# Retention attention feeding a top-2 mixture of experts: planner lanes, later expert weights, payloads stored by their own transfer, one-hots by token column

## The chip, the cores and the metric

The kernel runs on one core of a Trainium2 chip. The metric is the device time of one execution in microseconds (us). The core has five instruction queues that run in order, each for itself, and meet through semaphores: PE (matrix products), DVE (VectorE), ACT (ScalarE), POOL (GpSimd) and SP (SyncE, which here only issues transfers). ACT and POOL issue transfers as well. SP and ACT share eight completion semaphores for their transfers, used in turn: each transfer waits for the one eight places before it to land.

## The reference

Eight batches, eight heads, 576 positions, 64 numbers a head. The first part is attention without a softmax: scores fade with the distance by a fixed factor per head, and later positions are cut off. Its result, with the heads laid side by side, is the input `x` (4608 tokens of 512 numbers) of a mixture of eight experts, of which each token uses two.

```python
# attention
scores = scale * np.matmul(q, k.transpose(0, 1, 3, 2))
gamma = 1.0 - 2.0 ** (-5.0 - np.arange(H, dtype=np.float32))
Dmat = np.where(rel >= 0, gamma[:, None, None] ** rel[None, :, :], 0.0)
x = np.matmul(scores * Dmat, v)          # then (batch, position) x (head, d)
# experts
noisy_logits = x @ w_gate + np.log1p(np.exp(x @ w_noise)) * noise
top2 = np.argpartition(-noisy_logits, 2, axis=1)[:, :2]
top2_w = softmax over the two logits
for e in range(E):
    for k in range(2):
        mask = top2[:, k] == e
        h = np.maximum(x[mask] @ w1[e], 0.0)
        out[mask] += top2_w[mask, k, None] * (h @ w2[e])
```

Each expert has 512 x 1024 and 1024 x 512 weights (4 MB in f32, 33.5 MB for the eight).

## The kernel before

**The planner.** Nothing is issued as the code is read. `Plan.op` (L54-216) records each operation with the engines that may run it, an assumed cost, what it reads and writes, and a priority. `Plan.run` (L110) then plays the program through with these costs, picks for each operation the engine that would end it first, gives out buffers, and emits the operations in the order of the planned start times. That order is all that reaches the chip: each engine's queue runs in it, and semaphores keep the data right. `after=` makes the planner hold an operation back until another has ended by the plan; it adds no semaphore. So a change of an assumed cost or of `after` changes the order of instructions in the queues, and nothing else.

**The attention part** runs over 16 units; a unit is one batch and four heads, and four units make a batch pair. `load` (L377) issues five transfers of a unit on SP, 1.5 MB: k in two halves, q, v in two halves. `load_tail` (L395) fetches the last 64 positions of a batch pair in six transfers of 128 KB. `cast` (L406) turns them to bf16 on ACT, DVE and POOL (L420-L435), `tr` (L440) transposes on PE (L453), `scores` (L459, matmuls L478, mask on DVE L486), `states` (L493, L509) and `out_` (L521, L541 and L551) give x, transposed in `xT`. `tail` (L564) does the last 64 positions of a pair: casts on POOL (L578), transposes (L587), scores (L600), mask (L605).

**The routing** (`route`, L632) runs once for a batch pair, that is for 1152 tokens laid out as 128 partitions x 9 token columns, after the pair's last unit. Its steps in order: logits on PE (L652); exponential and logarithm on ACT (L658, L659); a chain of small DVE and POOL operations that picks the two best experts, ending in the one-hot of experts `MM` (L688); the payload `pay` of eight f32 a token (weights and indices, L695-L750); ranks within each expert by prefix-sum matmuls on PE (L716, L718); another chain on DVE (L725-L745) that turns a rank into a slot of the expert's list, split in a low part `lof` (0 to 127) and a high part `hif` (0 to 79). Then the list of tokens of each expert is built by matrix products. For each of the two choices j there is a one-hot `olo` of the low part (nine columns x 128, L757), a one-hot `oh` of the high part (nine columns x 80, L760), both on DVE in one instruction for all nine columns, and `oh` is multiplied by the token numbers `vals` (L763, on POOL or DVE). Nine matmuls per j sum olo^T oh (L769), and L776-L782 turn the sum into the int32 list `xi`.

The rows of x are stored to a table `xd` in device memory for later gathers. For each of five groups of token columns PE transposes them back (L793), ACT or DVE copies them to a buffer `xr` (L798), POOL or DVE copies the payload beside them (L799), and a transfer on ACT's queue stores both (L802): 264 numbers of f32 a row, 256 for x in bf16 pairs and 8 of payload.

**The experts.** `weights` (L851) brings experts 0 to 2 by casting transfers on POOL (L859, L863; four of 1 MB f32 each), held back in the plan until the loads of the units in `WAIT` have landed (L1122-L1124), and experts 3 to 7 on SP (L873, L876) with casts on ACT or DVE. Tokens of an expert are taken in tiles of up to two times 128. Nine tiles of experts 0 to 2 whose tokens are known early (`CLOSE`, `tiles` L882) run within the attention part, for pairs 0 to 2; the rest follows after pair 3's list. For each tile `fetch` (L903) gathers rows of `xd` on POOL (L913) and transposes them (L922); a gather waits for all row stores of the pairs that it may read (`xd_done`, in `record`, L1085). `up` (L961, matmuls L979), `down` (L999, L1014) follow; `finish` (L1047) scales the result by the token's weight on ACT (L1061) or DVE (L1063) and stores it to a table `yd` by SP (L1067), or, where it is a token's second expert, adds the first one's row (L1042 gathers it on POOL, L1071 adds on DVE) and scatters to the output on POOL (L1075).

Of the kernel before, what the change touches and what calls it, by code (L numbers as in the profile page):

```python
# [8 lines left out]
F32 = mybir.dt.float32  # L9
F16 = mybir.dt.float16  # L10
BF16 = mybir.dt.bfloat16
# [18 lines left out]
YOFF = [sum(min(-(-x // P) * P, CAP) for x in FIRST[:e]) for e in range(E + 1)]  # L30
WAIT = (8, 11, 14)
CLOSE = ((256, 0, 0, 0, 0, 0, 0, 0), (512, 384, 384, 0, 0, 0, 0, 0), (768, 640, 512, 0, 0, 0, 0, 0))
# [21 lines left out]
class Plan:  # L54
# [55 lines left out]
    def run(self):  # L110
        free, dma_free = {}, {}
        head = {k: 0 for k in self.fifo}
        used = {}
        ready = [o for o in self.ops if not o.need]
        order = []
# [24 lines left out]
        while ready:  # L140
            pick = None
            for o in ready:
# [76 lines left out]
class Kernel:  # L219
    def __init__(self, tc, ctx, src, gates, noise, w1, w2, out, xd, yd):  # L220
# [40 lines left out]
    def setup(self):  # L261
# [62 lines left out]
        for b in range(2):  # L324
# [49 lines left out]
    def unit(u):  # L374
        return u // 4, u // 2 % 2, u % 2

    def load(self, u):  # L377
        pl, nc = self.pl, self.nc
        bp, hq, b = self.unit(u)
        d = self.u[u] = {}  # L380
        for n in "kqv":
            t = d["raw" + n] = pl.buf("big", "att")
            s = self.src[n][2 * bp + b, 4 * hq:4 * hq + 4]
            if n == "q":
                pl.op("SP", 0.07, lambda e, s=s, t=t: nc.sync.dma_start(
                    out=t.t.rearrange("p (h x) -> p h x", h=4), in_=s[:, :512].rearrange("h (p r) d -> p h (r d)", r=4)),
                    w=[t], prio=u, dma=1.6)
            else:
                for c in range(2):
                    pl.op("SP", 0.07, lambda e, s=s, t=t, c=c: nc.sync.dma_start(  # L390
                        out=t.t.rearrange("p (c h x) -> p c h x", c=2, h=4)[:, c],
                        in_=s[:, 256 * c:256 * c + 256].rearrange("h (p r) d -> p h (r d)", r=2)),
                        w=[(t, c)], prio=u, dma=0.96)

    def load_tail(self, bp, prio):  # L395
        pl, nc = self.pl, self.nc
        d = self.tails[bp] = {}
        for n in "kqv":
            t = d["raw" + n] = pl.buf("half", "tl")
            for b in range(2):  # L400
                pl.op("SP", 0.07, lambda e, n=n, t=t, b=b: nc.sync.dma_start(
                    out=t.t[b * HD:(b + 1) * HD].rearrange("p (h d) -> p h d", h=E),
                    in_=self.src[n][2 * bp + b, :, 512:, :].rearrange("h s d -> s h d")),
                    w=[(t, b)], prio=prio, dma=0.8)

# [226 lines left out]
    def route(self, bp, prio):  # L632
# [104 lines left out]
        for j, op in ((0, Alu.add), (1, Alu.subtract)):  # L737
            o("DVE", DV, lambda e, j=j, op=op: V.tensor_tensor(gli.t[:, j], bt.t[:, j], t()[:, j], op), [bt, kt], [(gli, j)])
        lo, hi, lof, hif = f("lo", [P, 2, C], I32), f("hi", [P, 2, C], I32), f("lof", [P, 2, C], F16), f("hif", [P, 2, C], F16)
        ov = f("ov", [P, 2, C])  # L740
# [15 lines left out]
        for j in range(2):  # L756
            o("DVE", 1.3, lambda e, j=j: V.tensor_tensor(  # L757
                olo.t[:, j], iota.t.unsqueeze(1).to_broadcast([P, C, P]), lof.t[:, j].unsqueeze(2).to_broadcast([P, C, P]),
                Alu.is_equal), [iota, lof], [(olo, j)])
            o("DVE", 0.9, lambda e, j=j: V.tensor_tensor(  # L760
                oh.t[:, j], iota.t[:, :NH].unsqueeze(1).to_broadcast([P, C, NH]),
                hif.t[:, j].unsqueeze(2).to_broadcast([P, C, NH]), Alu.is_equal), [iota, hif], [(oh, j)])
            o({"DVE": 0.9, "POOL": 1.4}, 0, lambda e, j=j: self.eng(e).tensor_tensor(  # L763
                oh.t[:, j], oh.t[:, j], vals.t.unsqueeze(2).to_broadcast([P, C, NH]), Alu.mult), [vals, (oh, j)], [(oh, j)])
        pT = self.psum("rt")
# [19 lines left out]
        for g in ((0, 2), (2, 2), (4, 2), (6, 2), (8, 1)):  # L785
# [3 lines left out]
            def rows(e, c=c, n=n, p=p):  # L789
# [7 lines left out]
            o({"ACT": 0.17 + 0.43 * n, "DVE": 0.15 + 0.28 * n}, 0, lambda e, n=n, p=p, xr=xr: self.copy(  # L797
                e, xr.t.bitcast(BF16)[:, :n, :DM], p.t.bitcast(BF16).rearrange("p (c d) -> p c d", c=2)[:, :n]), [p], [(xr, 0)])  # L798
            o({"POOL": 0.3, "DVE": 0.2}, 0, lambda e, c=c, n=n, xr=xr: self.eng(e).tensor_copy(  # L799
                xr.t[:, :n, DM // 2:], pay.t[:, c:c + n, :]), [pay], [(xr, 1)])  # L800
# [284 lines left out]
    def record(self):  # L1085
        pl = self.pl
        self.u, self.tails, self.T, self.xT, self.W, self.t, self.keep, self.scats, self.wdma = {}, {}, {}, {}, {}, {}, {}, {}, []
        self.setup()
# [237 lines left out]
```

## Time and profile before

| | us |
|---|---|
| three runs | 522.32, 524.5, 525.01 |
| median | 524.5 |
| profiled execution | 519.78 |
| its span (first to last instruction) | 518.2 |
| mean granted PE clock in it | 0.927 |
| PE busy | 435.5 (84%) |
| POOL busy | 298.2 (58%) |
| DVE busy | 222.4 (43%) |
| ACT busy | 209.7 (40%) |

The span falls in two. From 0 to about 205 us run the 16 units, the four routings and the nine early tiles; pair 3's list is ready at 202 us. From there on PE has only the experts. In a timeline row the columns are the start, the duration of the group, the engine, the line, the operation, output<-input, shape and count, and in brackets the idle time of the engine before it and what ended it. In a waits row stand the waiting engine and line, what it waited for, and the total, the number of times and the longest, in us. A suffix q (SPq) means the engine's instruction queue: the time it was held at an instruction that only issues a transfer. "issue" is time for which the trace shows no cause.

### The profile page before, as it was taken

The numbers are of one execution on the slowest core, as the hardware profiler recorded it, in microseconds if no ns is written. First come the engines' busy times: TensorE is split into PE (matmuls) and PEld (weight loads), VectorE is DVE, ScalarE is ACT, GpSimd is POOL, SyncE is SP. The second block draws the span as 40 slices with busy tenths as digits, with TensorE's granted clock in tenths as the row PEclk, the third lists the DMA queues.
The fourth block names the chain that finished last, engine by engine and source line by source line (L and its number), as shares of the span: only waits on it lengthen the run. The fifth ranks groups of instructions, "written<-read, shape, count | busy, mean of one in ns | idle before, by whom it ended". The sixth has DMA issues, their size and how long they took to land.

```text
span 518.2 us, 12025 instructions
## 1 busy us (share of the span) xinstructions
PE 435.5 (84%) x4784; PEld 296.4 (57%) x4784; DVE 222.4 (43%) x535; ACT 209.7 (40%) x345; POOL 298.2 (58%) x355
## 2 busy tenths in 40 slices
PE   1887639876798899899999889989997799988993
PEld 1665527664576666567565546645645465654661
DVE  2465597793649359411515152341251121312132
ACT  3465425753565454345435334342441222322311
POOL 8846794795677527513253555546447366666453
PEclk9999757987969579999999999999999799999998
DMA  8999999999765314427679864885865333444333
GB/s 242 226 273 231 310 277 267 295 274 294 162 138 99 109 60 143 146 76 246 250 247 372 280 199 134 297 281 162 281 256 175 104 127 120 146 162 132 124 123 104
DMA packets 92125, 102.91 MB, mean 199 GB/s; under 512 B 21502, under 2 KB 70143, under 8 KB 92066
## 3 DMA queue, kind: packets, MB, share of 16 engines
q1 hardware_dynamic: 71874, 60.36, 38.7%
q0 software_dynamic: 15264, 36.89, 26.8%
q10 hardware_dynamic: 4928, 4.87, 2.8%
q8 instruction: 38, 0.62, 0.5%
q14 instruction: 21, 0.17, 0.1%
HBM read 83.20 MB, written 26.63 MB: 212 GB/s over the span
## 4 chain that ended last, share of the span: by engine, by line
PE 46%; issue 15%; POOL 11%; DMA 11%; DVE 7%; SPq 4%; ACT 3%; another core or an unknown queue 1%; POOLq 0%; ACTq 0%; DVEq 0%
PE ps L1014 15%; PE ps L979 14%; DMA xg<-xd,xi 4%; PE ps L509 4%; POOL xg L913 3%; DMA out_dram<-half,xg 3%; POOL half L1042 2%; DMA half<-in_q_dram 2%; PE ps L922 2%; PE ps L453 2%; PE ps L541 2%; PE ps L478 2%; POOL out_dram L1075 2%; SPq L390 2%; DMA big<-in_k_dram 1%
## 5 line engine op out<-in xcount | busy, mean ns | idle before, releaser
L979 PE MATMUL ps<-half,W 128*128 128x256 bf16 (+2 forms) x1344 | 221.2, 264 | 10.2 <-issue 6.1
L1014 PE MATMUL ps<-W,half 128*128 128x512 bf16 x624 | 222.7, 387 | 3.3 <-issue 1.8
L979 PEld LDWEIGHTS <-W 128*128 128x128 bf16 x1344 | 122.4, 98 | 79.9 <-issue 24.1
L993 ACT ACTIVATE half<-ps 128x512 bf16<-128x512 f32 (+2 forms) x160 | 87.1, 558 | 174.2 <-PE ps L979 108.8
L913 POOL DMA_INDIRECT xg<-xd,xi x80 | 83.2, 1040 | 104.9 <-DMA out_dram<-half,xg 24.9
L1014 PEld LDWEIGHTS <-half 128*128 128x128 bf16 x624 | 61.6, 100 | 34.0 <-issue 17.5
L1075 POOL DMA_INDIRECT out_dram<-half,xg x39 | 39.2, 1006 | 33.2 <-DVE half L1071 16.9
L1071 DVE SCALAR_TENSOR_TENSOR half<-ps,xg,half 128x512 f32<-128x512 f32 (+1 forms) x39 | 27.7, 745 | 68.0 <-issue 24.2
L1042 POOL DMA_INDIRECT half<-yd,xg x39 | 39.1, 1002 | 11.9 <-issue 11.6
L486 DVE TENSOR_TENSOR half<-ps,mask 128x512 bf16<-128x512 f32 x64 | 40.2, 708 | 6.5 <-ACT half L1061 3.2
L254 DVE COPY half<-ps 128x1024 bf16<-128x1024 bf16 (+2 forms) x47 | 30.9, 661 | 22.1 <-PE ps L922 8.7
L252 ACT ACTIVATE half<-ps 128x1024 bf16<-128x1024 bf16 (+2 forms) x31 | 29.4, 969 | 24.6 <-POOL oh L763 7.2
L428 POOL TENSOR_TENSOR half<-big,tab 128x1024 bf16<-128x1024 f32 x15 | 29.5, 1964 | 14.8 <-PE ps L551 5.9
L922 PE MATMUL ps<-ident__69,xg 128*128 128x128 bf16 (+1 forms) x320 | 28.7, 225 | 8.7 <-DMA xg<-xd,xi 7.4
L509 PE MATMUL ps<-half,half 64*64 64x64 bf16 (+2 forms) x512 | 32.4, 239 | 2.5 <-issue 1.9
L453 PE MATMUL ps<-ident__69,half 128*128 128x128 bf16 x256 | 24.9, 271 | 9.0 <-ACT half L420 6.0
L922 PEld LDWEIGHTS <-xg 128*128 128x128 bf16 (+1 forms) x320 | 21.4, 102 | 18.2 <-DMA xg<-xd,xi 10.0
L435 POOL TENSOR_TENSOR half<-big,tab 128x512 bf16<-128x512 f32 x26 | 28.4, 1106 | 0.5 <-issue 0.5
L509 PEld LDWEIGHTS <-half 128*64 128x64 bf16 (+1 forms) x512 | 20.1, 117 | 15.0 <-issue 7.2
L252 ACT ACTIVATE tb<-ps 64x512 bf16<-64x512 f32 x30 | 17.7, 591 | 26.4 <-PE ps L509 12.6
L1063 DVE TENSOR_SCALAR half<-ps,xg 128x512 f32<-128x512 f32 x9 | 6.8, 750 | 49.6 <-issue 32.7
L453 PEld LDWEIGHTS <-half 128*128 128x128 bf16 x256 | 21.3, 126 | 10.0 <-ACT half L420 6.0
(173 smaller groups left out, 436.9 us busy)
## 6 DMA issues: line engine op xcount, KB each, us to landing
big<-in_moe_w_dram SPq DMA_DIRECT2D x40, 512.0 KB
yd<-half SPq DMA_DIRECT2D x40, 256.0 KB
big<-in_k_dram SPq DMA_DIRECT2D x32, 256.0 KB
big<-in_q_dram SPq DMA_DIRECT2D x16, 512.0 KB
big<-in_v_dram SPq DMA_DIRECT2D x32, 256.0 KB
W<-in_moe_w_dram POOLq DMA_DIRECT2D x12, 512.0 KB
xd<-xr ACTq DMA_DIRECT2D x16, 264.0 KB
xg<-xd,xi POOLq DMA_INDIRECT x80
```

What stands on the lines that cost most here:

```text
L252: self.nc.scalar.activation(out, in_, Act.Copy)
L254: self.eng(e).tensor_copy(out, in_)
L453: nc.tensor.transpose(v[:, hp, x, :], i[:, y, hp * P:(hp + 1) * P], ident.t)
L486: nc.vector.tensor_tensor(S.t.bitcast(BF16).rearrange("p (h c x) -> p h c x", h=2, c=2)[:, h], p[h].t.rearrange("p (c x) -> p c x", c=2), ...
L509: nc.tensor.matmul(o[h * HD:(h + 1) * HD, hp, n, :], lhsT=kv[0][:k, r, c, 2 * hp + h, :], rhs=m, start=(hp == 0 and c == 0 and k == P and ...
L913: pl.op("POOL", 1.3, lambda _, x=x, h=h, n=n: nc.gpsimd.indirect_dma_start(out=x.t[:n, :], out_offset=None, in_=self.xd[:rows, :], in_offs ...
L922: nc.tensor.transpose(pv()[:, di, s * P:s * P + n], xb[:, di * P:(di + 1) * P], ident.t[:n, :n])
L979: nc.tensor.matmul(pv()[:, f2, :], lhsT=w.t[:, o:o + P], rhs=xv()[:, di, :n], start=(di == 0), stop=(di == KD - 1))
L993: nc.scalar.activation(hv(), pv(), Act.Relu)
L1014: nc.tensor.matmul(po[s].t[:n], lhsT=hv[:, s * P:s * P + n], rhs=w.t[:, o:o + DM], start=(f == 0), stop=(f == KF - 1))
L1042: pl.op("POOL", 1.3, lambda _, b=b, iy=iy, n=self.size(j): nc.gpsimd.indirect_dma_start(out=b.t[:n, :], out_offset=None, in_=self.yd[:rows ...
L1075: ins = nc.gpsimd.indirect_dma_start(out=self.out[:, :], out_offset=IOff(ap=io()[:n], axis=0), in_=o.t[:n, :], in_offset=None, bounds_chec ...
```

## The change

Five things change, the last two within the routing.

1. `WAIT` goes from the loads of units 8, 11 and 14 to those of 11, 14 and 15: the weights of experts 0, 1 and 2 are planned later.
2. The planner knows eight lanes of transfers that SP and ACT share, and eight of POOL's: by the plan a ninth transfer does not start before the one eight places earlier has landed.
3. A helper `inp` records the input loads; each is held back in the plan until the fifth load before it has landed.
4. `xr` loses its payload columns and L799 is gone. The payload goes from `pay` to `xd` by a transfer of its own per pair (1152 rows of 32 bytes); a gather waits for it as well. Row stores may be issued by ACT or SP, as the planner likes; it assumes 0.4 us on ACT and 0.07 on SP.
5. The one-hots are made one token column at a time by VectorE instructions whose second operand is a scalar per partition; the high one compares and multiplies by the token number in one instruction, so L763 is gone. For this `lof`, `hif` and `vals` become f32.

```diff
-WAIT = (8, 11, 14)
+WAIT = (11, 14, 15)
...
+        lanes = {"SP": [], "POOL": []}
+        lanes["ACT"] = lanes["SP"]
...
+                    if o.dma and len(lanes[e]) >= 8:
+                        t = max(t, lanes[e][-8])
...
+                lanes[e].append(o.fin)
...
-        pl.cls("xr", mk("xr", 5, [P, 2, XW], F32))
+        pl.cls("xr", mk("xr", 5, [P, 2, DM // 2], F32))
...
-        vals = f("vals", [P, C9], F16)
+        vals = f("vals", [P, C9])
...
+    def inp(self, fn, t, prio, dma):
+
+        self.inps.append(self.pl.op("SP", 0.07, fn, w=[t], prio=prio, dma=dma, after=self.inps[-5:-4]))
...
-            o("DVE", 1.3, lambda e, j=j: V.tensor_tensor(
-                olo.t[:, j], iota.t.unsqueeze(1).to_broadcast([P, C, P]), lof.t[:, j].unsqueeze(2).to_broadcast([P, C, P]),
-                Alu.is_equal), [iota, lof], [(olo, j)])
-            o("DVE", 0.9, lambda e, j=j: V.tensor_tensor(
-                oh.t[:, j], iota.t[:, :NH].unsqueeze(1).to_broadcast([P, C, NH]),
-                hif.t[:, j].unsqueeze(2).to_broadcast([P, C, NH]), Alu.is_equal), [iota, hif], [(oh, j)])
-            o({"DVE": 0.9, "POOL": 1.4}, 0, lambda e, j=j: self.eng(e).tensor_tensor(
-                oh.t[:, j], oh.t[:, j], vals.t.unsqueeze(2).to_broadcast([P, C, NH]), Alu.mult), [vals, (oh, j)], [(oh, j)])
+            def lows(e, j=j):
+                for c in range(C):
+                    V.tensor_scalar(olo.t[:, j, c], iota.t, lof.t[:, j, c:c + 1], None, Alu.is_equal)
+
+            def highs(e, j=j):
+                for c in range(C):
+                    V.tensor_scalar(oh.t[:, j, c], iota.t[:, :NH], hif.t[:, j, c:c + 1], vals.t[:, c:c + 1],
+                                    Alu.is_equal, Alu.mult)
+            o("DVE", 1.2, lows, [iota, lof], [(olo, j)])
+            o("DVE", 1.1, highs, [iota, hif, vals], [(oh, j)])
...
-            o({"POOL": 0.3, "DVE": 0.2}, 0, lambda e, c=c, n=n, xr=xr: self.eng(e).tensor_copy(
-                xr.t[:, :n, DM // 2:], pay.t[:, c:c + n, :]), [pay], [(xr, 1)])
...
-            pl.op("ACT", 0.4, lambda e, n=n, xr=xr, row=row: nc.scalar.dma_start(
-                out=self.xd[row:row + n * P, :].rearrange("(c p) w -> p c w", p=P), in_=xr.t[:, :n]),
+            pl.op({"ACT": 0.4, "SP": 0.07}, 0, lambda e, n=n, xr=xr, row=row: self.eng(e).dma_start(
+                out=self.xd[row:row + n * P, :DM // 2].rearrange("(c p) w -> p c w", p=P), in_=xr.t[:, :n]),
...
+        row = 1 + c0 * P
+        pl.op({"ACT": 0.4, "SP": 0.07}, 0, lambda e: self.eng(e).dma_start(
+            out=self.xd[row:row + C * P, DM // 2:].rearrange("(c p) w -> p c w", p=P), in_=pay.t),
+            r=[pay], w=[(self.xdk, (bp // 2, bp, "p"))], prio=prio, dma=1.4)
...
-        done = [(self.xdk, "d")] + [(self.xdk, (bp // 2, bp, c)) for bp in range(4) for c in (0, 2, 4, 6, 8)]
+        done = [(self.xdk, "d")] + [(self.xdk, (bp // 2, bp, c)) for bp in range(4) for c in (0, 2, 4, 6, 8, "p")]
```

What the built program shows of the order: all 20 row stores and the four payload stores are issued by SP, those of pair 0 among the loads of units 7 and 8, its payload ahead of half of unit 9's loads, those of pair 1 among and ahead of the loads of units 13 to 15, and two `yd` stores of expert 0's first tile (L1067) ahead of half of unit 14's v and all of unit 15. Before, no store stood ahead of an input load on SP. On PE the set of instructions is the same; the lists of pair 0 (L769), in two halves, now follow the scores of unit 6 instead of preceding them, the first tail's transposes go from unit 1 to unit 3, and the first tile of expert 0 goes from unit 10 to unit 11. The first half of expert 0's weights is issued on POOL just before pair 1's L695, the second after pair 1's L750; before, both stood in pair 0's routing and after it. The expert part after pair 3's list has the same order.

More of the change, by code (lines that the diff above doesn't have):

```diff
@@ L384, in load @@
             if n == "q":
-                pl.op("SP", 0.07, lambda e, s=s, t=t: nc.sync.dma_start(
+                self.inp(lambda e, s=s, t=t: nc.sync.dma_start(
                     out=t.t.rearrange("p (h x) -> p h x", h=4), in_=s[:, :512].rearrange("h (p r) d -> p h (r d)", r=4)),
-                    w=[t], prio=u, dma=1.6)
+                    t, u, 1.6)
             else:
                 for c in range(2):
-                    pl.op("SP", 0.07, lambda e, s=s, t=t, c=c: nc.sync.dma_start(
+                    self.inp(lambda e, s=s, t=t, c=c: nc.sync.dma_start(
                         out=t.t.rearrange("p (c h x) -> p c h x", c=2, h=4)[:, c],
                         in_=s[:, 256 * c:256 * c + 256].rearrange("h (p r) d -> p h (r d)", r=2)),
-                        w=[(t, c)], prio=u, dma=0.96)
+                        (t, c), u, 0.96)
     def load_tail(self, bp, prio):
@@ L400, in load_tail @@
             for b in range(2):
-                pl.op("SP", 0.07, lambda e, n=n, t=t, b=b: nc.sync.dma_start(
+                self.inp(lambda e, n=n, t=t, b=b: nc.sync.dma_start(
                     out=t.t[b * HD:(b + 1) * HD].rearrange("p (h d) -> p h d", h=E),
                     in_=self.src[n][2 * bp + b, :, 512:, :].rearrange("h s d -> s h d")),
-                    w=[(t, b)], prio=prio, dma=0.8)
+                    (t, b), prio, 0.8)
     def cast(self, u):
@@ L738, in route @@
             o("DVE", DV, lambda e, j=j, op=op: V.tensor_tensor(gli.t[:, j], bt.t[:, j], t()[:, j], op), [bt, kt], [(gli, j)])
-        lo, hi, lof, hif = f("lo", [P, 2, C], I32), f("hi", [P, 2, C], I32), f("lof", [P, 2, C], F16), f("hif", [P, 2, C], F16)
+        lo, hi, lof, hif = f("lo", [P, 2, C], I32), f("hi", [P, 2, C], I32), f("lof", [P, 2, C]), f("hif", [P, 2, C])
         ov = f("ov", [P, 2, C])
@@ L797, in route @@
             o({"ACT": 0.17 + 0.43 * n, "DVE": 0.15 + 0.28 * n}, 0, lambda e, n=n, p=p, xr=xr: self.copy(
-                e, xr.t.bitcast(BF16)[:, :n, :DM], p.t.bitcast(BF16).rearrange("p (c d) -> p c d", c=2)[:, :n]), [p], [(xr, 0)])
-            o({"POOL": 0.3, "DVE": 0.2}, 0, lambda e, c=c, n=n, xr=xr: self.eng(e).tensor_copy(
-                xr.t[:, :n, DM // 2:], pay.t[:, c:c + n, :]), [pay], [(xr, 1)])
+                e, xr.t.bitcast(BF16)[:, :n], p.t.bitcast(BF16).rearrange("p (c d) -> p c d", c=2)[:, :n]), [p], [(xr, 0)])
             row = 1 + (c0 + c) * P
-            pl.op("ACT", 0.4, lambda e, n=n, xr=xr, row=row: nc.scalar.dma_start(
-                out=self.xd[row:row + n * P, :].rearrange("(c p) w -> p c w", p=P), in_=xr.t[:, :n]),
+            pl.op({"ACT": 0.4, "SP": 0.07}, 0, lambda e, n=n, xr=xr, row=row: self.eng(e).dma_start(
+                out=self.xd[row:row + n * P, :DM // 2].rearrange("(c p) w -> p c w", p=P), in_=xr.t[:, :n]),
                 r=[xr], w=[(self.xdk, (bp // 2, bp, c))], prio=prio, dma=n * 0.4)
+        row = 1 + c0 * P
+        pl.op({"ACT": 0.4, "SP": 0.07}, 0, lambda e: self.eng(e).dma_start(
+            out=self.xd[row:row + C * P, DM // 2:].rearrange("(c p) w -> p c w", p=P), in_=pay.t),
+            r=[pay], w=[(self.xdk, (bp // 2, bp, "p"))], prio=prio, dma=1.4)
     def overflow_list(self, prio):
@@ L1086, in record @@
         pl = self.pl
-        self.u, self.tails, self.T, self.xT, self.W, self.t, self.keep, self.scats, self.wdma = {}, {}, {}, {}, {}, {}, {}, {}, []
+        self.u, self.tails, self.T, self.xT, self.W, self.t, self.keep, self.scats, self.wdma, self.inps = {}, {}, {}, {}, {}, {}, {}, {}, [], []
         self.setup()
```

## The prediction

> **What bounds the kernel now.** I read the table of stretches first, then PE's waits in the attention part, then timelines and the chain of waits around pair 0's routing, and last SP's waits. The columns of the first view are the stretch, its length, busy time (and groups) of PE, weight loads, DVE, ACT and POOL, the granted clock, the DMA share, GB/s.
>
> ```profile
> 50.00:75.00 25.00, 12.44 (x244) 10.20 (x244) 18.46 (x45) 7.45 (x13) 21.03 (x33) 0.64 1.12 298
> 75.00:100.00 25.00, 22.52 (x517) 17.66 (x515) 18.69 (x30) 16.29 (x26) 17.79 (x15) 0.81 1.17 272
> 100.00:125.00 25.00, 17.08 (x266) 14.36 (x267) 20.23 (x46) 10.08 (x17) 17.66 (x28) 0.80 1.13 289
> ...
> 205.00:300.00 95.00, 91.13 (x727) 58.66 (x724) 31.14 (x65) 42.92 (x74) 39.33 (x38) 1.00 0.68 227
> ```
>
> After 205 us PE is 96% busy and the change touches nothing there. Before, PE is half idle where a routing runs (12.44 of 25 us for pair 0, 17.08 for pair 1), with POOL and DVE the busiest. So what can be won lies in PE's waits up to 205 us:
>
> ```profile
> PE ps L769 <- POOL oh L763: 10.4, 4, 5.8
> PE ps L478 <- ACT half L252: 7.3, 5, 3.3
> ...
> PE ps L716 <- DVE MM L688: 4.1, 2, 3.4
> ...
> PE ps L587 <- POOL half L578: 3.1, 2, 2.9
> PE ps L769 <- DVE half L486: 2.6, 1, 2.6
> ```
>
> The largest is the list (L769) waiting for the one-hot that POOL multiplies. The chain shows why it is late in pair 0: POOL writes payload fields, issues weights, copies payloads, and only then multiplies.
>
> ```profile
> 67.06 1.25 POOL pay L750
> 68.32 0.08 POOL W L859
> 68.39 0.86 issue
> 69.26 0.76 POOL W L859
> 70.02 0.46 POOL xr L799
> 70.48 1.35 POOL oh L763
> 71.82 1.09 POOL xr L799 x3
> 72.91 1.36 POOL oh L763
> ```
>
> and VectorE beside it (start, duration):
>
> ```profile
> 68.26 0.90 DVE L760 TENSOR_TENSOR oh<-iota__66,hif 128x720 f16<-128x720 f16 x1
> 69.08 1.35 DVE L757 TENSOR_TENSOR olo<-iota__66,lof 128x1152 f16<-128x1152 f16 x1
> 70.35 2.25 DVE L760 TENSOR_TENSOR oh<-iota__66,hif 128x720 f16<-128x720 f16 x1
> ```
>
> The second L760 takes 2.25 us against 0.90, just while POOL runs L763: the two engines hold each other up.
>
> **What goes.** From PE's waits before 205 us I take those that belong to what is removed or moved: L769 on L763 10.4, L716 on L688 4.1, L587 on L578 3.1, L769 on L486 2.6; the tail's L600 on its two copies 1.1 and 0.8 and its L541 on L605 0.6; of the 7.3 of L478 the two behind a routing (1.20 at 76.28 us, 1.27 at 129.67); and 3.6 at L541 in pair 1, which waits for a copy on ACT that starts only after ACT's queue stood at three row stores (L802, 118.12 to 121.19 us), which go to SP. Sum: 10.4 + 4.1 + 3.1 + 2.6 + 1.1 + 0.8 + 0.6 + 2.5 + 3.6 = 28.8 us. All of it goes only if nothing takes its place: in PE's queue the waiting matmul now has others ahead of it, and what is still too late comes back below.
>
> **What comes back.** (a) Ranks. In pair 0 MM was ready 63.4 − 55.5 = 7.9 us after the logits' end; the matmuls that the new order puts in between last 6.9 us by their durations in this trace, so 1.0 stays. By the same reckoning 5.4 against 4.8 in pair 1 and 4.6 against 4.15 in pair 3: 2.0 us together.
>
> (b) Lists. The new operation is not in the trace: a VectorE instruction of 128x128 or 128x80 f16 with a scalar per partition. Nearest rows: a TENSOR_SCALAR of 128x80 (L779) lasts 0.24 us, and its successor starts 0.16 after it; the smallest, a memset of 128x1, lasts 0.059. [...] For VectorE's other work that stands between the 36 (masks L486, 0.68 each, at least four) I add 2.7. Pairs 2 and 3: nothing. Together 4.5.
>
> (c) VectorE against POOL. POOL's casts queued behind the routing (L428 1.91, L578 1.06) run beside the 36 instructions: 4.2 us of them in pair 0, 6 in pair 1, 2.1 in pair 2 by the order of the queue. If they held VectorE for all that time, 12.3 us, less the 4.4 that the same costs now (2.5 at L760 by its slow ones, 1.9 at L749, once 2.02 us instead of 0.17): +7.9. If not at all: −4.4. I take +3, nearer the upper end, since the L760 at 70.35 shows a hold about as long as POOL's instruction.
>
> [...]
>
> (d) Expert 0's weights. The last issue moves from 88.6 us to about 103 (pair 1's L750); its first up-product was at 106.6, 18 us after the last issue. The first tile moves on by a unit, 6.5 us (units 6 to 9 start scores at 76.3, 83.25, 89.0, 95.8). 0 if that and the gain of the queue's later place suffice, 6 if a unit's worth is missing; taken 2.
>
> (e) SP's queue. Two `yd` stores of expert 0's first tile stand ahead of half of unit 14's v and of unit 15. 0 if the tile ends in time, 6 in rival D below; taken 3.
>
> **What costs nothing, and its cover.** SP issues 24 more transfers of about 0.5 us, 12 us: covered, because loads are issued 40 us and more ahead of use (unit 12: issued from 90, scores at 137.2; unit 15: from 112, 172.1); without that cover the 12 us would stand before the scores. ACT loses 20 × 0.366 = 7.3 us of row stores, POOL 8 × 1.386 + 10 (L799) = 21; beyond the waits already counted PE waits for neither there. The payloads are 4 × 1152 packets more; at 45 ns of one engine each (queue q1: 71874 packets in 38.7% of 16 × 518 us) 13 us of all sixteen, 3.3 a pair, covered the same way; the two pairs before 125 us, where the DMA share is over 1.1, could push loads back by 6.6. The clock, 0.64 at 50 to 75 us, may rise when PE idles less: 0 to −4.5 (12.44 × 0.36), taken 0.
>
> **Sum.** 519.8 − 28.8 + 2.0 + 4.5 + 3 + 2 + 3 = 505.5 against the profiled execution's 519.78 (span 518.2 and 1.6 around it). The median of the runs lies 4.7 above that execution, so 510.
>
> **Rivals.**
>
> B, nearly the whole gain: (d) and (e) fit, and DVE's rows are cheap. 519.8 − 28.8 − 3 (half of (c)'s lower end and some of the clock's) + 4.7 = 493. For it: an undisturbed unit takes 6.5 us and a unit around a routing up to 23 (unit 5 to unit 6, 53.5 to 76.3). Against: pair 0's chain is long by itself.
>
> C, the same waits in other places (ranks, lists and tails wait for DVE and for loads instead of POOL): of 28.8 some 28 come back, 524. For it: DVE is busy 18.46 and 20.23 us of 25 in the routings' stretches, as much as POOL, and loses little. Against: the matmuls that now stand between.
>
> [...]
>
> D, slower: SP's queue in order, with stores ahead of loads. SP has stood at a load for a row store's landing before, since both engines' transfers share completion semaphores:
>
> ```profile
> SPq L401 <- DMA xd<-xr: 7.9, 1, 7.9
> ```
>
> That was harmless, because loads are early. Now the first tile's evictions (L1061) decide. They came 41 us after the last weight issue (88.6 to 129.5) and the second 9 later (138.3); with the issue at 103 they come at 144 and 153. From a load's issue to its scores it took 12.9 us at the least (unit 0, 0.97 to 13.88) and up to 60; with 25, unit 15's scores stand at 178 against 172.1 now. What the routings gained waits there, and 6 us are lost: 530. It decides, with the shortest lead, from an eviction later than 172.1 − 12.9 = 159, and for each us gained before it, one earlier. For it: row stores of pairs 1 and 2 stand in the same queue ahead of units 13 to 15. Against: if PE gains, the tile comes earlier too.
>
> That the change does nothing is excluded: the queues' order differs in the built program.
>
> **Chances.** Forecast 0.47; B 0.12; C 0.10; E 0.07; D 0.24. A measurement of this kernel tells ±0.5% of 524.5 from no change, 521.9 to 527.1. Faster: forecast, B and E, 0.66; same: C, 0.10; slower: D, 0.24. The forecast's own range, by the ends of (b) to (e) and the clock, is 499 to 519. The range for 8 in 10 leaves out half of B and the upper part of D: 490 to 531.
>
> **What would show it.** PE's waits at L769 and L716 below 7 us together; one-hots of 0.06 to 0.2 us each; PE busy over 15 of the 25 us from 50; pair 3's lists near 188 us instead of 202. I am wrong if L769 waits for the new instructions as long as for POOL before, if PE waits for unit 14's or 15's loads while SP stands at a store, or if the first tile waits for its weights.

## The result and the profile after

The changed kernel took 530.31 us (median; 529.44 to 532.06) beside 523.41 us for the kernel before: 1.0131 of it, 95% interval 1.009 to 1.0171. Two later series gave 1.0175 (1.0091 to 1.026) and 1.0112 (1.0074 to 1.015). It is slower; 510 was forecast, with "faster" at 0.66. The chips of the runs differ in speed (the kernel before takes 490 us on some, 520 to 524 on others), so each run is told as its ratio to the kernel before on the same chip.

The profiled execution took 530.5 us, its span is 529.0 (before 518.2). The medians lie only 6.9 us apart: the profiled execution of the kernel before was 3.6 us under its median, so the differences below are those of these two executions. Cut at the first score and at the last list of pair 3:

| us | before | after |
|---|---|---|
| start to first score | 13.9 | 15.6 |
| to pair 3's last list | 188.2 | 196.3 |
| of it PE busy / idle | 147.4 / 40.8 | 152.9 / 43.4 |
| experts behind it | 316.1 | 317.1 |

The 10.8 us are 1.7 at the start, 2.6 more idle time of PE, 5.5 more busy time, and 1.0 in the experts. So the loss lies where the change works. The busy time hides more waiting: the 72 list matmuls alone cover 12.5 us instead of 5.3, 7.2 more, although each by itself is shorter (212 ns on average, 241 before). They are spread out, as is shown below; without them PE is busy 1.7 us less than before.

By the first scores of units 5, 9, 12 and 15 one stage holds the loss. From unit 9 to unit 12, where pair 1's routing runs, it takes 54.1 us instead of 41.4; PE idles 6.0 us more in it and is busy 6.7 more, with 23 matmuls more and at the lower clock told below. The other four stages, from the first score to pair 3's last list, take 37.0, 44.3, 32.8 and 28.1 us instead of 39.6, 42.3, 34.9 and 30.0, together 4.6 less. The stretches of the changed kernel, with the columns as before:

```profile
50.00:75.00 25.00, 17.82 (x361) 14.03 (x358) 21.26 (x67) 11.82 (x21) 16.93 (x26) 0.77 0.93 252
75.00:100.00 25.00, 20.90 (x413) 16.38 (x412) 22.48 (x35) 13.75 (x21) 13.70 (x12) 0.69 0.93 245
100.00:125.00 25.00, 14.78 (x270) 10.00 (x267) 22.79 (x78) 11.13 (x17) 12.39 (x22) 0.73 0.81 174
```

From 50 to 75 us PE is busy 17.82 us instead of 12.44: pair 0's routing is filled, as forecast. From 75 to 125 it has 35.7 us instead of 39.6, and VectorE 45.3 instead of 38.9. The waits of PE up to 205 us:

```profile
PE ps L780 <- DVE oh L772: 14.5, 6, 7.2
PE ps L487 <- ACT half L257: 8.8, 6, 4.6
PE ps L725 <- DVE MM L697: 6.3, 4, 2.3
...
PE ps L462 <- DVE half L495: 3.6, 1, 3.6
```

L780 are the lists (L769 before) and now wait for VectorE's own one-hots, 14.5 us in place of 10.4 for POOL's multiply and 2.6 for a mask. The ranks wait 6.3 us in place of 4.1. The last row is new. Where it comes from is to be seen in the timelines of VectorE and of POOL in the changed kernel (start, duration):

```profile
83.93 7.87 DVE L431 TENSOR_SCALAR half<-big 128x1024 bf16<-128x1024 f32 x1
...
106.54 1.93 DVE L750 TENSOR_SCALAR lo<-gli 128x18 int32<-128x18 int32 x1
...
108.96 6.20 DVE L768 TENSOR_SCALAR olo<-iota__66,lof 128x128 f16<-128x128 f16 x9
115.08 1.98 DVE L772 TENSOR_SCALAR oh<-iota__66,hif,vals 128x80 f16<-128x80 f16 x9
...
117.05 1.54 DVE L768 TENSOR_SCALAR olo<-iota__66,lof 128x128 f16<-128x128 f16 x9
```

```profile
83.46 1.92 POOL L437 TENSOR_TENSOR half<-big,tab 128x1024 bf16<-128x1024 f32 x1
85.33 2.06 POOL L444 TENSOR_TENSOR half<-big,tab 128x512 bf16<-128x512 f32 x2
87.34 1.90 POOL L437 TENSOR_TENSOR half<-big,tab 128x1024 bf16<-128x1024 f32 x1
89.20 2.04 POOL L444 TENSOR_TENSOR half<-big,tab 128x512 bf16<-128x512 f32 x2
...
109.24 2.04 POOL L444 TENSOR_TENSOR half<-big,tab 128x512 bf16<-128x512 f32 x2
...
112.84 2.09 POOL L587 TENSOR_TENSOR half<-half,tab 128x512 bf16<-128x512 f32 x2
```

A cast of k on VectorE (L431) that takes 0.68 us elsewhere stands for 7.87 us: it starts 0.47 us after POOL's first cast and ends 0.56 us after the last of six that follow each other without a gap. Nine low one-hots take 6.20 us while POOL runs four casts and issues weights, and 1.54 us when POOL is idle. PE, behind both (timeline of PE, changed kernel; in brackets the wait before):

```profile
92.45 1.86 PE L462 MATMUL ps<-ident__69,half 128*128 128x128 bf16 x16 [3.65 <-DVE half L495]
...
115.42 1.91 PE L780 MATMUL ps<-oh,olo 128*128 128x80 f16 x9 [7.21 <-DVE oh L772]
```

The second row holds more than a wait: nine list matmuls take 1.91 us; in the kernel before they took 0.78 (115.93 us), at a granted clock of 0.50 (116 to 118 us). The clock is not the reason, for in **a_warm**, a run told below, nine of them take as long at a granted clock of 1.00 (118 to 120 us):

```profile
117.94 1.88 PE L785 MATMUL ps<-oh,olo 128*128 128x80 f16 x9 [1.60 <-DVE oh L772]
```

They follow VectorE's nine high one-hots (115.08 us, for 1.98 us in the rows above), one matmul behind each column, where before one instruction made all nine columns and the matmuls ran close together. In the other profiles too, the 72 list matmuls cover 10 to 14 us with the small one-hots and 4.7 to 5.8 with the large ones. So PE waits for VectorE ahead of the lists, and for 7.2 us more within them.

The granted clock is lower in that stage as well, 0.77 against 0.88 from unit 9 to unit 12, though up to pair 3's last list it is 0.82 against 0.83. First the changed kernel, then the kernel before, in two stretches of 8 us (the clock is the third number from the end):

```profile
108.00:116.00 8.00, 0.79 (x7) 0.39 (x5) 7.93 (x19) 3.02 (x4) 6.44 (x9) 0.69 0.46 61
116.00:124.00 8.00, 6.35 (x88) 3.91 (x88) 7.59 (x32) 1.08 (x2) 1.33 (x2) 0.50 1.07 227
```

```profile
108.00:116.00 8.00, 5.08 (x74) 3.78 (x74) 7.90 (x7) 3.44 (x6) 7.81 (x8) 0.95 1.12 251
116.00:124.00 8.00, 4.42 (x72) 4.17 (x73) 4.55 (x11) 1.19 (x2) 4.00 (x7) 0.71 1.14 319
```

Before, expert 0's first up-products ran in pair 1's gap (106.6 to 111); after, PE idles there, and then works at half its clock: 32 matmuls of L550 take 1.51 us at 120.70 us (granted clock 0.50 from 116 to 124), and 0.64 at 102.13 (1.00 from 102 to 103). In the changed kernel the clock is 1.00 from 104 to 108 us, 0.88 from 108 to 112 and 0.50 from 112 to 116, while PE waits 7.21 us for the lists, and 0.50 in the 8 us behind.

### The profile page after: what moved, and what is told of

Its sections match the earlier page's. It is cut to its first block, busy times and chain, and to the rows that moved or that the text cites. A ratio compares the mean times of both kernels' runs of the same rounds, so it can differ in the third digit from the quotient of the medians.

```text
span 529.0 us, 12069 instructions
## 1 busy us (share of the span) xinstructions
PE 439.7 (83%) x4742; PEld 295.4 (56%) x4784; DVE 231.1 (44%) x654; ACT 217.2 (41%) x350; POOL 273.9 (52%) x331
## 4 chain that ended last, share of the span: by engine, by line
PE 47%; issue 15%; DVE 11%; DMA 11%; POOL 7%; ACT 4%; SPq 3%; another core or an unknown queue 1%; POOLq 0%; DVEq 0%; ACTq 0%
PE ps L992 17%; PE ps L1027 15%; DMA xg<-xd,xi 3%; DMA big<-in_v_dram 3%; DVE olo L768 3%; PE ps L518 3%; POOL half L1055 2%; DMA big<-in_moe_w_dram 2%; PE ps L935 2%; DVE oh L772 2%; ACT half L257 2%; PE ps L462 2%; POOL xg L926 2%; PE ps L487 2%; POOL out_dram L1088 1%
## 5 line engine op out<-in xcount | busy, mean ns | idle before, releaser
L992 PE MATMUL ps<-half,W 128*128 128x256 bf16 (+2 forms) x1344 | 224.3, 267 | 13.8 <-issue 6.0
L1027 PE MATMUL ps<-W,half 128*128 128x512 bf16 (+1 forms) x582 | 210.4, 387 | 8.9 <-issue 4.4
L1006 ACT ACTIVATE half<-ps 128x512 bf16<-128x512 f32 (+2 forms) x156 | 85.1, 557 | 175.9 <-PE ps L992 100.8
L1027 PEld LDWEIGHTS <-half 128*128 128x128 bf16 x624 | 61.6, 99 | 30.0 <-issue 15.0
L1055 POOL DMA_INDIRECT half<-yd,xg x39 | 38.9, 998 | 11.9 <-issue 11.6
L257 ACT ACTIVATE half<-ps 128x1024 bf16<-128x1024 bf16 (+2 forms) x39 | 37.8, 1000 | 17.1 <-PE ps L935 6.8
L462 PE MATMUL ps<-ident__69,half 128*128 128x128 bf16 x256 | 23.9, 259 | 15.6 <-ACT half L429 6.0
L444 POOL TENSOR_TENSOR half<-big,tab 128x512 bf16<-128x512 f32 x31 | 31.9, 1047 | 5.7 <-DMA big<-in_v_dram 4.0
L257 ACT ACTIVATE xT<-ps 128x512 bf16<-128x512 f32 (+1 forms) x39 | 19.5, 555 | 29.4 <-PE ps L560 20.6
L935 PE MATMUL ps<-ident__69,xg 128*128 128x128 bf16 (+1 forms) x320 | 26.8, 220 | 3.6 <-DMA xg<-xd,xi 2.4
L462 PEld LDWEIGHTS <-half 128*128 128x128 bf16 x256 | 19.3, 117 | 17.9 <-issue 7.8
L259 DVE COPY half<-ps 128x1024 bf16<-128x1024 bf16 (+2 forms) x39 | 25.0, 642 | 7.9 <-issue 4.1
```

Of the source, the lines that this page charges most:

```text
L257: self.nc.scalar.activation(out, in_, Act.Copy)
L444: self.eng(e).tensor_tensor(o, i, t, Alu.mult)
L462: nc.tensor.transpose(v[:, hp, x, :], i[:, y, hp * P:(hp + 1) * P], ident.t)
L935: nc.tensor.transpose(pv()[:, di, s * P:s * P + n], xb[:, di * P:(di + 1) * P], ident.t[:n, :n])
L992: nc.tensor.matmul(pv()[:, f2, :], lhsT=w.t[:, o:o + P], rhs=xv()[:, di, :n], start=(di == 0), stop=(di == KD - 1))
L1006: nc.scalar.activation(hv(), pv(), Act.Relu)
```

## The experiments

Three theories stood at the outset. V: VectorE's one-hots, in their own time and in holds by POOL. W: expert 0's weights come too late, so that nothing fills pair 1's routing. S: SP stands at `yd` stores ahead of units 14 and 15.

### One part undone, or one other route

**a_wait.**

```diff
-WAIT = (11, 14, 15)
+WAIT = (8, 11, 14)
```

> The changed kernel (530.3 us) with the weights' hold-back at the loads of units 8, 11, 14 again, all else kept. In the built order expert 0's first up-products then stand between pair 1's ranks and its lists, where PE was idle for 7.2 us at L780 in the changed kernel. Theory W (the first tile no longer fills pair 1's routing, and everything behind it is a unit later): about 7 us of that wait are filled and the first tile's end no longer holds SP's queue, 518 to 523. Theory V (VectorE's one-hots and GpSimd's holds cost the time): the lists are as late as before, only the filler helps, 526 to 529. Theory S (SP's queue stands at the yd stores): those stores still stand ahead of units 14 and 15 but are ready some 20 us earlier, 522 to 526.

Measured 1.0047 (1.0009 to 1.0085). The up-products stand in pair 1's gap again and the lists still come at 117.2 us. Against the changed kernel, 1.0112 on a chip of that speed, some 0.6% come back. That is 525.9 us at the speed of the first chip: between the ranges of W and V, and within that of S.

**a_big.** Same order, large instructions.

```diff
-                for c in range(C):
-                    V.tensor_scalar(olo.t[:, j, c], iota.t, lof.t[:, j, c:c + 1], None, Alu.is_equal)
+                V.tensor_tensor(olo.t[:, j], iota.t.unsqueeze(1).to_broadcast([P, C, P]),
+                                lof.t[:, j].unsqueeze(2).to_broadcast([P, C, P]), Alu.is_equal)
...
+                V.tensor_tensor(oh.t[:, j], oh.t[:, j], vals.t.unsqueeze(2).to_broadcast([P, C, NH]), Alu.mult)
```

> The changed kernel with the same planned costs, so with the same order on every engine, but each one-hot made by one instruction over all nine columns (f16 operands) and the product with the token numbers by a third large instruction on VectorE: 3 in place of 18 per choice. Their own time by the profile before is 1.35 + 0.90 + 0.90 = 3.15 us a choice, against 1.54 + 1.98 = 3.52 undisturbed in the changed kernel. Theory V in its narrow form (eighteen small instructions give GpSimd eighteen chances to come in between): the nine low one-hots of pair 1 go from 6.20 us to under 3.5, and the time falls by 3 to 5 us, 525 to 527. If what matters is only that VectorE does this work while GpSimd's casts run, however it is cut, the total stays within 2 us, 528 to 531. Theories W and S: no change.

> The changed kernel's order with three large one-hot instructions a choice in place of eighteen small ones, a second time, now beside the changed kernel. Narrow theory V: 0.8 to 1.2% less than the changed kernel. If it is within 0.4% of it, the cutting into small instructions isn't what costs.

Measured 1.0032 (0.9995 to 1.0069), and the second time 1.0015 (0.9974 to 1.0056) beside 1.0175 for the changed kernel. By the ratios 1.6% come back, by the medians of that series 0.7% (522.69 and 526.32 us); that chip scattered widely, so the size stays open. The profile of a_big shows less than this: the low one-hots of pair 1 take 1.36 us instead of 6.20, but a high one is held for 3.20, the lists still wait for VectorE, and the second one of pair 1 comes at 121.4 us. The cut into small instructions costs something, and it is not all.

**a_yd.**

```diff
-                pl.op("SP", 0.07, lambda _, y=y, r0=r0, n=n: nc.sync.dma_start(out=self.yd[r0:r0 + n, :], in_=y.t[:n]),
-                      r=[y], w=[(key, j)], prio=prio, dma=0.7)
+                early = t[2] < 3
+                pl.op("ACT" if early else "SP", 0.4 if early else 0.07, lambda g, y=y, r0=r0, n=n: self.eng(g).dma_start(
+                    out=self.yd[r0:r0 + n, :], in_=y.t[:n]), r=[y], w=[(key, j)], prio=prio, dma=0.7)
```

> The changed kernel with the yd stores of the early tiles issued by ACT instead of SP; no store of results stands ahead of an input load any more. Theory S: SP no longer stands for 21.7 us from 125.5 us on, the loads of units 14 and 15 are issued by 130 us, the 10 us for v of unit 15 on the chain are gone, 518 to 524. Theories W and V: the loads are early, but what is late are pair 1's lists and the first tile, 527 to 531.

Measured 1.02 (1.0138 to 1.0262). The loads of unit 15's k and q are issued at 129 to 134 us instead of 149 to 151, and nothing is won; scores of unit 15 start at 180.9 us, 177.6 in the changed kernel on a chip of that speed. But v of unit 15 comes no earlier, because SP now stands 15.0 us at a row store (L811) that precedes it:

```profile
149.25 0.37 SPq L811 DMA_DIRECT2D xd<-xr  x1
149.66 0.46 SPq L399 DMA_DIRECT2D big<-in_v_dram  x1
```

So a_yd clears the `yd` stores and not SP's queue as a whole. In the changed kernel SP does stand at a `yd` store:

```profile
124.81 0.73 SPq L399 DMA_DIRECT2D big<-in_v_dram  x1
147.37 0.34 SPq L1080 DMA_DIRECT2D yd<-half  x1
147.75 0.43 SPq L399 DMA_DIRECT2D big<-in_v_dram  x1
```

What it holds up are loads of units 14 and 15, and the loss lies before unit 12's scores; from there to unit 15's scores the changed kernel takes 2.1 us less than the kernel before. So S is not the loss. It may still take back a part of that gain: POOL waits 3.8 us for the last half of v (until 166.1 us), ahead of pair 2's routing in its queue, and a run with v ahead of both kinds of stores was not made.

**a_pace.** No lanes, no `inp`.

```diff
-        lanes = {"SP": [], "POOL": []}
-        lanes["ACT"] = lanes["SP"]
...
-        self.inps.append(self.pl.op("SP", 0.07, fn, w=[t], prio=prio, dma=dma, after=self.inps[-5:-4]))
...
```

> The changed kernel without the planner's eight lanes and without the paced input loads; the weights' hold-back, the payload's own transfer and the one-hots stay as changed. The order of the first six units is again that before: pair 0's lists stand ahead of unit 6's scores. If the pacing gained what unit 6 shows (59.2 us instead of 76.3, 4 us of it still there at unit 8), this is slower than the changed kernel by some 4 us, 533 to 537. If the pacing is the loss (row stores among the loads, the longer hold of the k cast at 84 us), 522 to 526.

Measured 1.0023 (0.9978 to 1.0067), about 0.9% below the changed kernel (1.0112 at that speed). Pair 0's lists stand ahead of unit 6 again, its scores start at 78.0 us, and the time is less: the gain in pair 0 is lost later.

### One part alone, on the kernel before

**b_hot, b_wait, b_pay, b_pace** take the one-hots, the later weights, the payload's transfer and the pacing each alone from the diff shown above.

> The kernel before (523.4 us) with the one-hots by token column alone. VectorE's own work is 7.0 us a pair instead of 4.5, GpSimd loses the multiply. In the built order expert 0's up-products stand between pair 1's ranks and lists. Theory V: the lists are held by GpSimd's casts as in the changed kernel, 526 to 530. Theories W and S: this part is not at fault; the wait of PE for L763 (10.4 us) goes for the most part, 516 to 522.

> The kernel before with the weights' hold-back at the loads of units 11, 14 and 15 alone. In the built order the first up-products stand between the two halves of pair 1's list instead of behind its ranks. Theory W: the first tile is late by a unit or more and pair 1's routing stands unfilled, 528 to 533. Theories V and S: within 2 us of before, 522 to 526.

> The kernel before with the payload's own transfer alone, row stores on the engine that the planner picks (all on SP among the loads). No yd store stands ahead of an input load here. Theory S in its wide form (any store among the loads in SP's queue holds them): 526 to 531, with SP standing over 15 us at row and payload stores before 175 us. Theories W and V: 520 to 524, since 20 payload copies are gone from GpSimd and the row stores from ACT.

> The kernel before with the planner's eight lanes and the paced input loads alone. In the built order pair 0's lists follow unit 6, expert 0's up-products fill pair 1's routing, and two yd stores stand ahead of part of unit 14's and all of unit 15's loads. If the pacing is a gain by itself, 512 to 519 (PE's 7.5 us for pair 0's lists filled). Theory S: the yd stores hold the loads as in the changed kernel and take it back, 522 to 528.

| part alone | ratio | interval |
|---|---|---|
| one-hots by column | 1.0121 | 1.0028 to 1.0215 |
| later weights | 0.9895 | 0.9816 to 0.9974 |
| payload's own transfer | 0.9934 | 0.9876 to 0.9991 |
| pacing | 1.0012 | 0.9968 to 1.0056 |

W falls as a cause by itself: later weights alone gain 1%, although pair 1's gap is nearly as empty (PE 2.3 us busy from 108 to 116; 0.8 in the changed kernel). In the changed kernel's order they may still cost the 0.6% of a_wait. The payload's transfer gains 0.7% with all row stores among SP's loads, so S in its wide form is not the loss either. The one-hots alone lose 1.2%.

### The one-hots undone, on one chip with the changed kernel

**after_again** is the changed kernel, **a_hot** has the old one-hots and f16 operands, **a_big_wait** joins a_big and a_wait.

> The changed kernel unchanged, so that the others of this series stand beside it on one chip; the first four experiments ran on a chip on which the kernel before takes 490 us, not 524. Theory V (VectorE's one-hots) and theory W (late weights) have no different numbers here: 1.009 to 1.017 of before as measured first. Should it come out at 1.002 to 1.005, as three of the undoings did there, these say nothing of the parts that they undo.

> The changed kernel with the one-hots of the kernel before: large instructions, the product on GpSimd, planned at the old costs (the order of the lists shifts by a unit in places). Theory V in any form: the loss is gone, 0.995 to 1.003 of before. Theory W: pair 1's routing is as empty as in the changed kernel, 1.008 to 1.015.

> The changed kernel with large one-hot instructions on VectorE and the weights' hold-back at units 8, 11, 14 again; the rest as changed. If V and W are both parts of the loss, this lies below each undone alone (1.003 and 1.005 on the first chip): 0.985 to 0.998 of before. If one of them is no part of it, it stays with the better one, 1.000 to 1.005.

Measured 1.0175, 0.9964 (0.9927 to 1.0001) and 1.016 (1.0121 to 1.0199). Without the new one-hots the loss is gone. The last is a miss: both undone together are worse than each. Its order is that of a_wait; a compare of the high one-hot stands for 6.32 us at 68.6 us there. Most edits make a new order, and which instructions it puts beside each other matters; the parts do not add up.

### The holds

**a_kact** moves one instruction.

```diff
         def k(e):
+            if u == 10:
+                e = "ACT"
```

**a_hot_kact** has this and the old one-hots. **after_third** is the changed kernel beside them.

> The changed kernel once more, as the measure for the three beside it on this chip: 1.009 to 1.026 of before by the two series so far. No theory differs here.

> The changed kernel with one cast of k (unit 10's, which stands at 83.93 us for 7.87 us on VectorE while GpSimd runs six casts back to back) issued to ACT; nothing else moves in any queue but this instruction. Theory H (VectorE's SBUF instruction is held by GpSimd's until it pauses): no VectorE instruction over 3 us is left there, PE's idle time at 88 to 92 us goes from 3.65 us to under 1, pair 1's ranks come 3 to 6 us earlier, and 0.5 to 1.1% of the time goes. Rival (the hold is hidden by pair 1's routing, which waits for other things): less than 0.3%.

> The changed kernel with the one-hots of the kernel before (0.9964 of before by itself, with the same hold, 8.44 us at 82.2 us) and the one cast on ACT. Theory H: 0.985 to 0.992 of before, the best so far with the whole of the rest of the change. Rival: 0.993 to 1.000.

Measured 1.0112 (1.0074 to 1.015) for the changed kernel, 0.999 (0.996 to 1.0021) for a_kact, 0.9881 (0.9815 to 0.9947) for a_hot_kact. One instruction of 0.68 us, taken from VectorE where POOL runs its six casts, is worth 1.2%. PE and ACT in a_kact, where the changed kernel waited 3.65 us (timelines):

```profile
90.15 1.07 PE L464 MATMUL ps<-ident__69,half 128*128 128x128 bf16 x16
```

```profile
86.56 1.06 ACT L431 ACTIVATE half<-big 128x1024 bf16<-128x1024 f32 x1
```

PE does not wait there, pair 1's ranks start at 99.6 us instead of 104.3 in after_third, and pair 3's last list at 196.1 instead of 200.4. On top of it the old one-hots are worth another 1.1%.

**a_warm** fills PE's wait.

```diff
         def table(e, j):
+            if bp == 1 and j == 0:
+                idb = self.fixed["ident"].t
+                for _ in range(26):
+                    nc.tensor.matmul(pT.t, lhsT=idb, rhs=idb.unsqueeze(1).to_broadcast([P, 4, P]),
+                                     start=True, stop=True, skip_group_check=True)
```

> The changed kernel with 26 matmuls of 128x512 more, whose result is overwritten, ahead of the first list matmul of pair 1: PE runs them in the 7.2 us in which it waits at L780 for VectorE, the order is otherwise the same. Theory K (PE's wait costs a second time, since the granted clock is 0.50 in the 8 us behind it, 116 to 124 us, against 0.71 in the kernel before): the clock behind the lists stays above 0.8 and the span to pair 3's lists falls by 3 to 6 us, 0.6 to 1.1% below the changed kernel. Rival (the wait alone costs, the clock is low for another reason): the clock behind it stays near 0.5 and the time is the changed kernel's within 0.4%, or more if the added matmuls delay the list.

Measured 1.01 (1.004 to 1.0161), beside 1.0112: no gain. The stretches in a_warm:

```profile
116.00:124.00 8.00, 4.61 (x37) 2.23 (x39) 8.00 (x34) 0.00 (x0) 1.65 (x3) 0.81 1.10 195
124.00:132.00 8.00, 8.00 (x126) 6.27 (x118) 2.11 (x7) 2.32 (x5) 5.20 (x6) 0.55 1.04 306
```

The clock is 0.81 from 116 to 124 us and not 0.50, as theory K says, but it falls within that stretch, and is 0.55 where the changed kernel has 0.95 (after_third, 124 to 132). In windows of 2 us it is at half from about 121 to 131 us, in after_third from about 111 to 125. So the low clock came 10 us later and was not gone: PE still waits 1.60 and 1.55 us ahead of the two lists of pair 1 and follows VectorE's one-hots within them. Keeping PE busy with empty work at this place buys nothing. That does not refute theory K, since most of the low clock stayed; why it falls there, with no wait of PE over 1.60 us ahead, is open.

### Which parts make the hold, and the best version

**c_wp** is the kernel before with the later weights and the payload's transfer only; **a_hot_kact2** repeats the best until then.

> The kernel before with the late weights (units 11, 14, 15) and the payload's own transfer, without the pacing and with the old one-hots. Each alone gave 0.9895 and 0.9934. If the pacing's order is what puts GpSimd's six casts back to back beside VectorE's cast of k, no VectorE instruction over 4 us stands at 80 to 95 us here and the two gains add up in part: 0.980 to 0.990 of before. If the hold comes with the late weights or the payload (they take the transfers out of GpSimd's queue between the casts), it is here as well: 0.993 to 1.000.

> The best version so far (old one-hots, all the rest of the change, one cast of k on ACT; 0.9881 with 0.9815 to 0.9947) a second time beside it. 0.982 to 0.995 if the gain holds on another chip, and then below or above the version without the pacing by what the pacing is worth.

Measured 0.9748 (0.9673 to 0.9823) for c_wp, 478.28 us beside 491.63, and 0.9861 (0.977 to 0.9952) for the other. c_wp is the best version. VectorE's longest instruction near the place is

```profile
84.02 2.33 DVE L422 TENSOR_SCALAR half<-big 128x1024 bf16<-128x1024 f32 x1
```

The hold of about 8 us is in every kernel with both the pacing and the late weights in which the cast is on VectorE (the changed kernel 7.87, a_big 7.87, a_yd 7.86, a_hot 8.44, a_warm 7.87), and in none with one of the two (the longest at 80 to 95 us: a_wait 1.44, a_pace 2.40, b_pace 1.06, b_wait 2.40). So it belongs to the order that the two make together. By the timelines POOL's queue then has gathers and casts only, which come free at once; in the kernel before weight issues stand among them (78.4 and 88.6 us). That this is the reason was not tried. Other holds come without them, 6.20 us in b_hot (L435 at 92.3) and 4.65 in b_pay (L422 at 130.2). Between a_hot (0.9964, another chip) and c_wp lies the pacing with its hold; without the hold (a_hot_kact2) the pacing still costs about 1%, whose place was not looked for.

## Why the prediction was wrong

- **What goes: 28.8 us of waits.** The same waits are there again with another name at the end: lists 13.0 before, 14.5 after, and 7.2 more between the list matmuls; ranks 4.1 and 6.3; copies ahead of scores 7.3 and 8.8. Only the tail's transposes (3.1) and L541's 3.6 went for the most part. This is the step that failed: the waits were taken out whole, and what came back was priced at 6.5 us (ranks 2.0, lists 4.5), though VectorE, which the lists and the ranks now wait for, had little room (18.46 and 20.23 us of 25). The first of the prediction's signs of being wrong came true: the lists wait for the new instructions as long as for POOL before.
- **(b) Lists, 4.5 us.** No run shows the part of the term that stands for the one-hots' cost, nor the term's ends: they were the author's estimate. The changed kernel shows 2 × (1.54 + 1.98) = 7.0 us for a pair's one-hots undisturbed: an instruction of 128x128 with one scalar lasts 0.24 us and its successor starts 0.16 after it, one of 128x80 with two scalars 0.29 and 0.21. From pair 1's ranks (103.84) to its list (115.42) PE had 4 us of matmuls, at the full clock then (1.00 from 103.8 to 108), and waited 7.21, more than the 4.5 for all four pairs.
- **(c) Holds, +3 between −4.4 and +7.9.** That POOL's casts hold VectorE was right and the size was not; the upper end was nearer. VectorE's instructions from the ranks on took, in the routings of pairs 0 to 2, 13.6 us longer than their shortest (3.3 + 7.9 + 2.4), somewhat above the 12.3 of a full hold, and the cast of k 7.2 more, which was on no list, since only casts beside the one-hots were looked at. By a_kact that one cast costs 1.2%.
- **(d) Late weights, +2.** On the kernel before it has the wrong sign: alone −1.05%, and −2.5% with the payload's transfer. In the changed kernel's order the sign may be right, as a_wait wins some 0.6% by taking them back (3 us, on another chip than the run beside it).
- **(e) SP's queue, +3, and rival D.** SP stood at the `yd` store from 125.5 to 147.4 us, near the times that D worked out, but the stage in which it could cost, from unit 12 to unit 15, is 2.1 us shorter than before. What the trace still shows of it is POOL's wait of 3.8 us for v. That D's 530 is what was measured is chance.
- **The clock, 0.** Right for the whole: 0.82 against 0.83 up to pair 3's last list, and 1.7 us less busy time without the list matmuls. It was lower where the loss lies (0.77 against 0.88) and no higher at 52.6 to 96.9 us, around pair 0's routing (0.70; before 0.71).
- **Hidden transfers and payload packets.** By the sum right: b_pay gains 0.7%.
- What happened is nearest to rival C, with 7.0 us of one-hots a pair, and those held: the waits come back on VectorE. C was given 0.10 and has too small a sum (524 against 530.31), since it held no cast outside the routing; E, the rival with dear one-hots, was given 0.07.

## What to carry to other kernels

When work moves from GpSimd to VectorE, list every VectorE instruction that will stand beside a run of GpSimd instructions without gaps, not only the moved one, and let it count as long as the run (here 7.87 us for a cast of 0.68). A wait was not removed here by putting other matmuls ahead of it, since the engine that ends it had no room (VectorE was busy 22.79 us of 25 from 100 to 125 us in the changed kernel, and the lists waited for it 14.5 us in all); compare its busy time in that stretch first. Try each part of a bundle alone: here two parts gained 2.5% and the other two took it back and more.

## What the runs showed of the hardware

- One VectorE instruction can be held through several GpSimd instructions in a row: 7.87 us for one of 0.68 in the changed kernel, six casts long, and 8.44 in a_hot. In the kernel before, a hold went either way: VectorE's L760 took 2.25 us instead of 0.90 at 70.35 us beside POOL's L763 (1.38, as elsewhere), and L763 took 2.43 instead of 1.39 at 112.08 us beside VectorE's L757 (1.35).
- Thirty-six small one-hots a pair, 7.0 us undisturbed on VectorE, against four large ones of 4.5 (2 × 1.35 + 2 × 0.90) and two multiplies of 1.39 on POOL: an instruction with a scalar per partition over 128 f16 elements lasts 0.24 us and its successor starts 0.16 after it; with two scalars over 80 elements 0.29 and 0.21. The one of fewer elements is the slower:

```profile
L768 DVE TENSOR_SCALAR olo<-iota__66,lof x72: 242/244/2556, 66.8 to 209.7; 128x128 f16<-128x128 f16 x72
```

```profile
L772 DVE TENSOR_SCALAR oh<-iota__66,hif,vals x72: 292/295/1889, 70.0 to 211.5; 128x80 f16<-128x80 f16 x72
```

(lines of the changed kernel: shortest, median and longest in ns, first and last start).
- The granted clock behind 7.2 us of idling was 0.50 for 8 us; with the gap filled it was 0.81 there and 0.55 in the next 8 us, and fell with no wait of PE over 1.60 us ahead of it.
- Busy time of PE can hide waiting: nine list matmuls that follow nine one-hots, 0.21 us from start to start, cover 1.9 us at a granted clock of 0.50 (the changed kernel) and of 1.00 (a_warm), and 0.78 us where their input is ready (the kernel before, at 0.50).
